# Attention scores issued before the PV that frees their slots, a PV that stops early, and a convolution that keeps instruction words in reserve

## The chip, the cores and the metric

One core of one Trainium2 chip runs the whole kernel. The metric is the device time of one execution in microseconds (us). The core has a tensor engine (PE; its weight loads are shown as PEld), a vector engine (DVE), a scalar engine (ACT), a general engine (POOL) and a queue engine (SP). The engines run their own instruction streams and wait for each other by semaphores.

## The reference

Two independent blocks share one launch, and their results stand side by side in the output. Block A is attention with 32 heads of 16 dimensions over 2048 rows; block B is a gated long convolution (written with FFTs in the reference, computed as a causal convolution here).

```python
# A: x (1, 2048, 512), wqkv (512, 1536), wo (512, 512), bfloat16
q, k, v = split_heads(x @ wqkv)                 # 32 heads, Dh = 16
scores = einsum("bhqd,bhkd->bhqk", q, k) * Dh ** -0.5
o = einsum("bhqk,bhkd->bhqd", softmax(scores), v)
a = merge_heads(o) @ wo
# B: q, k, v (1, 2048, 512), shift_k (512, 4), ssm_k (512, 2048), ssm_D (512)
kv = causal_conv4(k, shift_k) * v
y = causal_conv2048(kv, ssm_k) + kv * ssm_D
b = q * y
return concatenate([a, b], axis=-1)
```

The softmax needs 32 x 2048 x 2048 exponentials. They are the bulk of the work that is not matrix multiplication.

## The kernel before

**Tiles.** Attention is cut into 32 groups (8 groups of 4 heads by 4 blocks of 512 queries), each group into 16 key tiles of 128 and 4 heads: 2048 blocks of 128 keys by 512 queries. For one block PE computes the scores into one PSUM bank (`qk_mm`, L829), the exponential is taken, and PE multiplies the result with V (`emit_pv`, L966, called PV) and adds it into bank `PVB`. Four blocks whose heads lie in four different row strips make one set of four matmuls that run side by side.

**Two engines take exponentials.** ACT takes most blocks, two or three at a time (one instruction of 1024 or 1536 columns, L856, output in the ring `PT` of 19 slots). DVE takes the others by integer tricks: one pass out of PSUM (L892, output in the ring `PTD`), then three passes over two blocks together (L918, L923, L927).

**Steps.** The main loop counts steps `T`. A step issues the scores of its two or three ACT blocks and often of one DVE block (`emit_qk`), the ACT instruction that reads them, PV of blocks of two and more steps ago (`pv_step`), and then background work (`emit_bg`): the projections of Q, K, V and of the output, and the convolution (`conv_lags`, L1236), which is 8192 small matmuls in "lags" of four. Filler matmuls (`warm_up`, L1487) are put where PE would be idle for long, and `keep_busy` (L1493) once the convolution is done. The score banks are used in turns: the scores of step `T` wait until the ACT instruction of step `T-2` has read the same banks.

**The order is fixed when the program is built.** A planner in Python keeps a model of each engine's time and decides, step by step, what each engine's stream holds; nothing is decided on the chip. So a change of a rule moves instructions all through the program. Three rules matter here.

- `pv_make_room(T)` (L999): if one of the three `PT` slots that come next is still held by a block without its PV, PV is forced (`pv_step(T, True)`). The main loop calls it ahead of `emit_qk(T)`, so the forced PV stands before the scores of step `T` in PE's stream. Forced PV goes on through all blocks that are ready.
- `pv_step` without force issues every set of ready blocks that is full enough; nothing compares it with the time at which the next scores are due.
- PE's instructions arrive in blocks of 256 words (a matmul with its weight load is 2 words). The planner's model of PE (`Tensor`) notes when the next block is expected to land. `spare()` gives how many words of the present block may be used: what is left of it less `NEED` (12) words for each us until the landing. The convolution takes at most `spare() / 8` lags in a step, and the fillers ask it too.

Of the kernel before, what the change touches and what calls it, by code (L numbers as in the profile page):

```python
# [26 lines left out]
C = 512  # L27
# [11 lines left out]
PVB = 6  # L39
BGB = 7  # L40
# [3 lines left out]
LAGS = 14  # L44
# [17 lines left out]
N_TAIL = 10  # L62
# [3 lines left out]
R_PTD = 10  # L66
# [30 lines left out]
MARGIN = 0.2  # L97
QN_T = 4
PV_WAIT = 0.1
PV_AGAIN = 1  # L100
SPARE = 0
DMA_KB = 394
# [14 lines left out]
WAIT = 1  # L117
LATE = 0.2
V512 = (0.60, 0.726)
V4 = (0.20, 0.326), (0.334, 0.46)  # L120
V2 = (0.334, 0.46), (0.60, 0.726)
SAME = 0.012
SWITCH = 0.105
LANDS = 0.115
MM = 0.216
LAG = 0.0555
# [4 lines left out]
LOADED = 1.3  # L131
WR_KB = 310
NEED = 12.0
FILL = 0.054


# [73 lines left out]
class Tensor(Eng):  # L210
# [45 lines left out]
        end = max([b for a, b in self.loads[-12:] if a <= cross + ISSUED], default=0.0)  # L256
        return max(cross + FETCH, end + LOADED)

    def spare(self):
        need = max(self.lands - self.t, 0.0) * NEED  # L260
        return BLOCK - self.at_word % BLOCK - need if need else 10 ** 6


# [11 lines left out]
def bass_concat_heads__mha_block__ssm_conv_h3__prompt_kernel(  # L275
# [76 lines left out]
    pe = Tensor(sem("s_pe"), done)  # L352
# [3 lines left out]
    def at(*deps):  # L356
        return pe.at(deps)
# [127 lines left out]
    bank_free = {b: None for b in range(8)}  # L485
# [226 lines left out]
    NL = NQB * NG - 1  # L712
# [31 lines left out]
    late = {"bank": None}  # L744

    end = [10 ** 6]
# [27 lines left out]
    h_exp = {}  # L774
# [14 lines left out]
    def emit_qk(T):  # L789
        banks = take_banks(T)  # L790
        bl, extra = next_blocks(T, len(banks)) if len(queue) > LAST_BLKS else (queue[:2], None)
        d_bank = [hold(T, banks)] if extra is not None else []
        banks_of[T] = banks = banks[:len(bl)]
        chunks[T] = bl + [extra] * len(d_bank)
        for b in chunks[T]:
            queue.remove(b)
            chunk_of[b] = T
        on = list(zip(chunks[T], banks + d_bank))
        more = []
        if late["bank"] in banks and len(on) > 2:  # L800
            more = [on.pop(banks.index(late["bank"]))]
        h = qk_mm(on)
        if extra is not None:
            on_dve[extra] = len(on_dve)
            exp_on_dve(extra, d_bank[0], h)
        if more:
            if at(bank_free[more[0][1]]) + 0.13 > pe.t + 0.1:
                advance(pe.t)
                pv_take(T)
                pv_step(T)  # L810
            h = qk_mm(more)
        h_exp[T] = emit_exp(bl, banks, h)

    def qk_mm(on):
# [48 lines left out]
    pt_used, pt_of, pt_free = {}, {}, {}  # L863

    def pt_next():
        p = pt_at[0]
        return set(range(p, min(p + MOST, R_PT))) | (set(range(MOST)) if p + MOST > R_PT else set())
# [21 lines left out]
    def exp_on_dve(b, bank, h):  # L889
        i = on_dve[b]  # L890
        fix_u = PTD[:, i % R_PTD, 0, :].bitcast(U16)
        h_f = urgent(lambda e: e.tensor_scalar(fix_u, PS[:, bank, :], FIX_ADD, FIX_HI, ALU.add, ALU.min),  # L892
                     [h, h_ptd.get(i - R_PTD)], slack=S_FX)
        bank_free[bank] = h_f
        if waits and i % R_PTD:
            passes(waits.pop() + [b], i - 1, h_f)
        else:
            settle()
            waits.append([b])
            fixed[0] = h_f  # L900

    waits, fixed = [], [None]

    def settle():
        if waits:
            bl = waits.pop()
            passes(bl, on_dve[bl[0]], fixed[0])
# [29 lines left out]
    pv_n = {}  # L937
# [55 lines left out]
    def pv_make_room(T):  # L993
        pv_take(T)
        for i in range(2):
            p, need = pt_at[0], set()
            for n in (3,):
                p = 0 if p + n > R_PT else p
                need |= set(range(p, p + n))  # L999
                p += n  # L1000
            if not need & set(pt_used):
                return
            advance(pe.t)
            pv_step(T, True)

    acts, dves = [], []
    pv_seen = set()
# [12 lines left out]
            else:  # L1020
                acts.append((b, 0))

    def pv_step(T, force=False):
        pv_unit(T, force)
        if pv_part[0] is not None:
            return
        for n, j in sorted({sub(b) for b, part in acts + dves}):
            if n > 0 and pv_done.get(n - 1, T) >= T + force or j > 0 and not conv_done() or j > 1 and sub_done.get(j - 2, T) >= T:
                break
            a = [x for x in acts if sub(x[0]) == (n, j) and all((OF[n], kt // 4) in h_v for kt, q0, w in tiles(x[0]))]  # L1030
            d = [x for x in dves if sub(x[0]) == (n, j)]
            own = [i for i in range(4 * KT * n, 4 * KT * (n + 1)) if sub(i) == (n, j)]
            close = all(i in chunk_of for i in own) and T >= max(chunk_of[i] for i in own) + 2
            late = close and (T >= max(chunk_of[i] for i in own) + (NL_PV if n == NL and j < 3 else 2 if n == NL else LAST_PV) or force)
            if late:
                for b, part in d:
                    if b not in h_blk and waits and b in waits[0]:
                        settle()
                    while b not in h_blk:
                        k = dve.n  # L1040
                        advance(pick()[0] + 0.01)
                        assert dve.n > k
            d = [x for x in d if x[0] in h_blk and (late or at(h_blk[x[0]]) <= pe.t - (0.0 if close else LATE))]
            bl = a + d
            if bl and PV_WAIT and not force and n > 0 and T < end[0] - N_TAIL and not any(pv_n.get((n, i)) for i in range(4)) and at(bank_free[PVB]) + 0.13 > pe.t + pe.turn("C") + PV_WAIT:
                break
            while bl:
                run = []
                for x in bl:
                    if blk(x[0])[2] not in [blk(y[0])[2] for y in run]:  # L1050
                        run.append(x)
                old = [x for x in run if x[0] not in on_dve and pt_of[x[0]] in pt_next()]
                if len(run) < 4 and not close and not old and len([x for x in bl if x[0] in on_dve]) < DV_MIN and T < end[0]:
                    break
                for x in run:
                    bl.remove(x)
                    (dves if x[0] in on_dve else acts).remove(x)
                emit_pv(run, T)

    def finish_group(n, h, T):  # L1060
        dt = DT[:, :]
# [63 lines left out]
    h_wop = [None]  # L1125
# [168 lines left out]
    def room(T):  # L1294
        lim = at(h_exp[min(T, end[0] - 1)]) - 0.47 - MARGIN
        return lim - max(pe.t, at(bank_free[BGB]))
# [110 lines left out]
    def emit_bg(T):  # L1407
        st = state
        now[0] = T
        unit_step(T)  # L1410
        if T == N_OPEN:
            assert not early
            st["started"], st["t"] = True, pe.t
        if T >= end[0] - N_TAIL:
            tail_step(T)
            return
        if conv_done():
            if h_wop[0] is not None and not any(pv_n.get((NL, i, 128)) for i in range(4)):
                bank_free[BGB] = pe.op(keep_busy, [bank_free[BGB], h_wop[0]], run=MM, kind="F")
            return  # L1420
        if not st["started"] or alone[0] or at_rest() and (part[0] or st["turn"] or next_unit(T) is not None):
            return
        left_us = max(STEP_US * (PLAN - END - T) - JOB_US * len(jobs), 1.0)
        st["lags"] = min(st["lags"] + min(PACE * st["left"] / left_us, RATE) * (pe.t - st["t"]), CAP)
        st["t"] = pe.t
        left = min(LAGS, int(st["lags"]), int((room(T) - pe.turn("C") - SWITCH) / LAG), int(pe.spare() / 8))
        while left > 0 and st["qd"] < wr_next[0] and h_kvc[st["qd"] // 16] is not None and at(h_kvc[st["qd"] // 16]) + WAIT <= pe.t and at(h_wr[st["qd"]]) + WAIT <= pe.t:
            n0 = st["lag"]
            if n0 == 0 and st["qd"] % 4 == st["from"] and at(bank_free[BGB]) > pe.t - 0.2:
                break  # L1430
            n1 = min(n0 + left, NLAG)
            left -= n1 - n0
            st["lags"] -= n1 - n0
            st["left"] -= n1 - n0
            conv_lags(st["qd"], n0, n1)
            st["lag"] = n1 % NLAG
            if n1 == NLAG:
                st["qd"] += 1
                if st["qd"] % 4 == 0:
                    st["turn"] = True  # L1440
                if st["qd"] % 4 == st["from"]:
                    break
# [93 lines left out]
    T = 0  # L1536
    while T < end[0] + 3:
        if T < end[0]:
            pv_make_room(T)
            emit_qk(T)  # L1540
        advance(pe.t)
        alone[0] = full_step(T)
        pv_take(T)
        if not alone[0]:
            pv_step(T)
        advance(pe.t)
        emit_bg(T)
        warm_up(T)
        advance(pe.t)
        T += 1  # L1550
# [75 lines left out]
```

## Time and profile before

| | us |
|---|---|
| three timed executions | 749.92, 746.77, 749.25; median 749.25 |
| the profiled execution | 750.88 |
| its span, from the first to the last instruction | 749.1 |
| ACT busy in the span | 724.8 |
| PE busy, DVE busy | 703.4, 702.0 |

The mean granted TensorE clock is 0.991 of full speed. The profiled execution took 1.6 us more than the median. An engine's busy time is the union of its instructions; successive ACT instructions overlap in the records, so a sum of their durations is more than the busy time. A name such as "PT<-PS" says which tile is written and which is read.

### The profile page before, as it was taken

How to read it: one execution, taken by the hardware profiler on the slowest of the kernel's cores; microseconds unless marked ns; L12 is line 12 of the kernel's file. 1: busy time of each engine (PE TensorE's matmuls, PEld its weight loads, DVE VectorE, ACT ScalarE, POOL GpSimd, SP SyncE). 2: the span in 40 equal slices, each digit the busy share in tenths (PEclk: the TensorE clock that was granted, in tenths of full speed). 3: DMA queues.
4: the chain of work that ended last, by engine and by line, in shares of the span. 5: the costliest groups of instructions: out<-in, count | busy, mean ns of one | idle time of the engine just before them, and what ended most of it. 6: DMA issues, size and time to landing. Idle time of an engine off the chain costs nothing.

```text
span 749.1 us, 32530 instructions
## 1 busy us (share of the span) xinstructions
PE 703.4 (94%) x14696; PEld 315.4 (42%) x14696; DVE 702.0 (94%) x1437; ACT 724.8 (97%) x690; POOL 98.7 (13%) x172
## 2 busy tenths in 40 slices
PE   7999899999989999999999999999999999899997
PEld 3334344445443444444434344443443443344344
DVE  3999999999989999999899998999999997899995
ACT  6999999999989999999999999999999999899997
POOL 7202102020202002020021301120011201210000
PEclk9999999999999999999999999999999999999999
DMA  9797767677775787775576577575898566666210
GB/s 201 201 260 262 226 199 232 242 248 233 252 232 178 229 282 259 255 234 200 160 266 202 184 253 236 200 255 189 297 287 249 185 208 207 231 200 230 90 39 30
DMA packets 73720, 161.48 MB, mean 216 GB/s; under 512 B 34064, under 2 KB 37776, under 8 KB 73200
## 3 DMA queue, kind: packets, MB, share of 16 engines
q1 hardware_dynamic: 66400, 150.43, 62.0%
q0 software_dynamic: 5984, 8.66, 3.8%
q8 instruction: 116, 1.90, 1.0%
q10 hardware_dynamic: 1200, 0.33, 0.2%
q14 instruction: 20, 0.16, 0.1%
HBM read 142.61 MB, written 6.42 MB: 199 GB/s over the span
## 4 chain that ended last, share of the span: by engine, by line
ACT 60%; DVE 27%; PE 11%; issue 1%; DMA 1%; POOL 0%
ACT PT L856 60%; DVE PTD L892 11%; DVE PTD L923 5%; PE PS L829 4%; PE PS L966 4%; DVE PTD L918 3%; DVE PTD L927 3%; PE PS L1236 2%; DVE DT L1064 1%; DMA xT<-in_A_x_dram 1%; PE PS L516 1%; DVE KV L604 1%; PE PS L1493 1%; DVE OUTA L1149 1%; DVE QN L1271 0%
## 5 line engine op out<-in xcount | busy, mean ns | idle before, releaser
L856 ACT ACTIVATE PT<-PS 128x1024 bf16<-128x1024 f32 (+2 forms) x686 | 722.6, 1290 | 13.4 <-PE PS L829 13.0
L892 DVE TENSOR_SCALAR PTD<-PS 128x512 uint16<-128x512 f32 x464 | 309.8, 680 | 19.7 <-PE PS L829 18.6
L829 PE MATMUL PS<-QT,KTo 32*128 32x512 bf16 (+2 forms) x2248 | 271.6, 367 | 26.1 <-ACT PT L856 15.4
L966 PE MATMUL PS<-PT,VA 128*32 128x512 bf16 (+2 forms) x1748 | 181.2, 369 | 4.5 <-DVE PTD L923 1.4
L1236 PE MATMUL PS<-WR,KV 128*24 128x128 bf16 (+8 forms) x8192 | 182.6, 221 | 1.9 <-issue 1.9
L1236 PEld LDWEIGHTS PS<-WR,KV 128*32 128x32 bf16 (+7 forms) x8192 | 136.0, 95 | 58.7 <-issue 36.0
L923 DVE TENSOR_TENSOR PTD<-PTD 128x1024 f16<-128x1024 f16 x232 | 154.9, 678 | 0.3
L829 PEld LDWEIGHTS PS<-QT,KTo 32*128 32x128 bf16 x2248 | 71.2, 91 | 195.8 <-ACT PT L856 138.3
L966 PE MATMUL PS<-PTD,VA 128*32 128x512 f16 (+1 forms) x1000 | 152.9, 370 | 0.5 <-DVE PTD L927 0.4
L369 POOL DMA_DIRECT2D QT<-QS x120 | 61.2, 517 | 398.0 <-DVE QS L582 374.2
L927 DVE TENSOR_SCALAR PTD<-PTD 128x1024 uint16<-128x1024 uint16 x232 | 94.8, 414 | 0.3
L918 DVE TENSOR_SCALAR PTD<-PTD 128x1024 uint16<-128x1024 uint16 x232 | 92.2, 415 | 0.3
L966 PEld LDWEIGHTS PS<-PT,VA 128*32 128x32 bf16 x1748 | 45.6, 94 | 89.9 <-issue 71.0
L966 PEld LDWEIGHTS PS<-PTD,VA 128*32 128x32 bf16 x1000 | 38.6, 95 | 12.5 <-issue 1.6
L1487 PE MATMUL PS<-IDN,ZW 128*32 128x512 bf16 (+3 forms) x178 | 42.6, 307 | 0.3 <-DVE DT L1064 0.2
L369 POOL DMA_DIRECT2D out_dram<-OUTA x15 | 8.8, 586 | 109.3 <-DVE OUTA L1149 109.3
L1064 DVE STREAM_TRANSPOSE DT<-PS 128x512 f32<-128x512 f32 x31 | 21.9, 707 | 0.6 <-PE PS L966 0.5
L570 PE MATMUL PS<-WKV,xT 128*128 128x128 bf16 x256 | 19.3, 220 | 1.1 <-DVE KTo L591 0.5
L516 PE MATMUL PS<-xT,WQ 128*32 128x512 bf16 x240 | 18.3, 384 | 1.2 <-DVE DT L1064 0.7
L516 PE MATMUL PS<-xT,WKV 128*32 128x512 bf16 (+1 forms) x256 | 18.2, 376 | 0.8 <-DVE QN L1271 0.5
L1487 PEld LDWEIGHTS PS<-IDN,ZW 128*32 128x32 bf16 x178 | 13.2, 95 | 12.7 <-issue 8.1
L570 PEld LDWEIGHTS PS<-WKV,xT 128*128 128x128 bf16 x256 | 14.4, 98 | 8.8 <-issue 3.6
(72 smaller groups left out, 246.7 us busy)
## 6 DMA issues: line engine op xcount, KB each, us to landing
WR<-kz_scratch SPq DMA_DIRECT2D x256, 512.0 KB, 5.3
KV<-KV SPq DMA_DIRECT2D x16, 256.0 KB, 5.2
kz_scratch<-WR SPq DMA_DIRECT2D x1, 2176.0 KB, 8.3
QN<-in_B_q_dram POOLq DMA_DIRECT2D x8, 256.0 KB, 5.3
out_dram<-QN POOLq DMA_DIRECT2D x8, 256.0 KB, 2.9
QT<-QS POOLq DMA_DIRECT2D x120, 16.0 KB, 4.4
out_dram<-OUTA POOLq DMA_DIRECT2D x15, 128.0 KB, 2.7
QN<-in_B_ssm_k_dram SPq DMA_DIRECT2D x1, 1024.0 KB, 8.0
```

The costliest lines, as they stand in the source:

```text
L369: f(outp, inp).then_inc(dsem.sem, 16)
L516: ins = e.matmul(dst[g:g + 32], lhsT=w[:, g:g + 32], rhs=rhs, tile_position=(0, g), **kw)
L570: ins = e.matmul(PS[:, bank, 128 * j:128 * j + 128], lhsT=xT[:, dc, (4 * sc + j) * 128:(4 * sc + j + 1) * 128], rhs=WV[:, dc, o * 128:(o + ...
L829: ins = e.matmul(PS[:, bank, i * w:i * w + w], lhsT=KTo[32 * s:32 * s + 32, OF[n_] % 2, kt * 128:(kt + 1) * 128], rhs=QT[32 * s:32 * s + 3 ...
L856: h = act.op(lambda e: e.activation(PT[:, p0:p0 + n, :], src, ACT.Exp, scale=EXP_SCALE, bias=EXP_BIAS), [h, free], us=(0.065 + 0.4257 * n, ...
L892: h_f = urgent(lambda e: e.tensor_scalar(fix_u, PS[:, bank, :], FIX_ADD, FIX_HI, ALU.add, ALU.min), [h, h_ptd.get(i - R_PTD)], slack=S_FX)
L918: st["h"] = dve.op(lambda e: e.tensor_scalar(mant_u, fix_u, MANT, HALF_BITS, ALU.bitwise_and, ALU.bitwise_or), [st["h"]], us=us)
L923: st["h"] = dve.op(lambda e: e.tensor_tensor(mant, fix, mant, ALU.mult), [st["h"]], us=us)
L927: h = dve.op(lambda e: e.tensor_scalar(fix_u, fix_u, OCTAVE, ONE_MORE, ALU.bitwise_and, ALU.bitwise_or), [st["h"]], us=us)
L966: ins = e.matmul(dst, lhsT=w, rhs=rhs, start=first, stop=last, tile_position=(0, 32 * s))
L1236: ins = e.matmul(PS[32 * g:32 * g + 2 * ((30 - d) // 2 + 1), BGB, 128 * kk:128 * kk + w], lhsT=kv, rhs=WR[:, r + g, S - 64 * d - 128:S - 6 ...
L1487: pe.op(lambda e, s=s, k=k, rhs=rhs, bank=bank, rows=rows, c0=c0, first=first: e.matmul(PS[32 * s:32 * s + rows, bank, c0:c0 + 128 * k], l ...
```

## The change

- `pv_make_room(T)` moves out of the main loop into `emit_qk`: now behind the scores of step `T` and ahead of the ACT instruction that writes into the freed slots. Forced PV stops as soon as the slots are free (`enough`).
- `pv_step` without force returns when the next set of PV would put PE's time more than `PV_OVER` (0.2 us) past the time at which the scores that follow are due by the model.
- The convolution's reserve is `NEED_C` = 17 words for each us to the landing instead of 12. The fillers keep 12.
- `keep_busy` is put in only if its bank is free already.
- The passes of DVE blocks are written for a general number of blocks together, `WIDE`. It is 2, as before, and the first two entries of the planner's tables `V4` and `V2` are the old ones to a thousandth.

```diff
+PV_OVER = 0.2
+WIDE = 2
+NEED_C = 17.0
@@ Tensor
-    def spare(self):
-        need = max(self.lands - self.t, 0.0) * NEED
+    def spare(self, rate=NEED):
+        need = max(self.lands - self.t, 0.0) * rate
@@ emit_qk
             h = qk_mm(more)
+        pv_make_room(T)
         h_exp[T] = emit_exp(bl, banks, h)
@@ exp_on_dve
-        if waits and i % R_PTD:
-            passes(waits.pop() + [b], i - 1, h_f)
-        else:
+        if waits and i % R_PTD == 0:
             settle()
-            waits.append([b])
-            fixed[0] = h_f
+        if not waits:
+            waits.append([])
+        waits[0].append(b)
+        fixed[0] = h_f
+        if len(waits[0]) == WIDE:
+            settle()
@@ pv_make_room
-            pv_step(T, True)
+            pv_step(T, True, lambda: not need & set(pt_used))
@@ pv_step
-    def pv_step(T, force=False):
+    def pv_step(T, force=False, enough=lambda: False):
...
+                if not force and not late and T < end[0] - N_TAIL and max(pe.t, at(bank_free[PVB]) if not any(pv_n.get((n, i)) for i in range(4)) else 0.0) + pe.turn("C") + MM > at(h_exp[T]) - 0.47 + PV_OVER:
+                    return
...
                 emit_pv(run, T)
+                if enough():
+                    return
@@ emit_bg
-            if h_wop[0] is not None and not any(pv_n.get((NL, i, 128)) for i in range(4)):
+            if h_wop[0] is not None and not any(pv_n.get((NL, i, 128)) for i in range(4)) and at(bank_free[BGB]) <= pe.t:
...
-        left = min(LAGS, int(st["lags"]), int((room(T) - pe.turn("C") - SWITCH) / LAG), int(pe.spare() / 8))
+        left = min(LAGS, int(st["lags"]), int((room(T) - pe.turn("C") - SWITCH) / LAG), int(pe.spare(NEED_C) / 8))
@@ main loop
-            pv_make_room(T)
             emit_qk(T)
```

What this does to the streams can be read from the built programs. L829 and L966 of before are L833 and L972 in the changed kernel, L1236 is L1246, and L1487 is L1497.

The first place is PE's stream where PV is forced, some 543 us into the span of the kernel before. QT,KTo names scores, WR,KV the convolution, PT,VA and PTD,VA are PV of ACT's and of DVE's blocks.

```order
L829 MATMUL PS<-QT,KTo 128x512 x3
L1236 MATMUL PS<-WR,KV 16x128 x4
L1236 MATMUL PS<-WR,KV 14x128 x8
L1236 MATMUL PS<-WR,KV 12x128 x8
L1236 MATMUL PS<-WR,KV 10x128 x8
L1236 MATMUL PS<-WR,KV 8x128 x4
L966 MATMUL PS<-PT,VA 32x512 x15
L966 MATMUL PS<-PTD,VA 32x512 x5
L829 MATMUL PS<-QT,KTo 128x512 x3
L1236 MATMUL PS<-WR,KV 8x128 x4
```

One of the forced PVs in PE's stream of the changed kernel:

```order
L833 MATMUL PS<-QT,KTo 128x512 x3
L1246 MATMUL PS<-WR,KV 22x128 x4
L1246 MATMUL PS<-WR,KV 20x128 x8
L1246 MATMUL PS<-WR,KV 18x128 x8
L1246 MATMUL PS<-WR,KV 16x128 x8
L1246 MATMUL PS<-WR,KV 14x128 x8
L833 MATMUL PS<-QT,KTo 128x512 x3
L972 MATMUL PS<-PT,VA 32x512 x12
L1246 MATMUL PS<-WR,KV 12x128 x8
```

Before, 32 matmuls of the convolution and 20 of PV stand between two sets of scores. Now only the convolution does, and PV follows the scores. The ACT instruction of that step waits for the first four PV matmuls behind its scores, which free its slots. Eight ACT instructions of the changed kernel wait in this way; in the kernel before none waits for a PV.

The second place lies two steps behind the first difference of the two programs (there the convolution's 12x128 x8 was taken out): PE's stream where the kernel before is some 87 to 92 us into its span. IDN,ZW names fillers. Before:

```order
L829 MATMUL PS<-QT,KTo 128x512 x3
L966 MATMUL PS<-PT,VA 32x512 x2
L966 MATMUL PS<-PTD,VA 32x512 x2
L829 MATMUL PS<-QT,KTo 128x512 x6
L966 MATMUL PS<-PT,VA 32x512 x5
L966 MATMUL PS<-PTD,VA 32x512
L1236 MATMUL PS<-WR,KV 10x128 x4
L829 MATMUL PS<-QT,KTo 128x512 x6
L966 MATMUL PS<-PT,VA 32x512 x3
L966 MATMUL PS<-PTD,VA 32x512
L966 MATMUL PS<-PT,VA 32x512
L966 MATMUL PS<-PTD,VA 32x512 x3
```

The same place in the changed kernel:

```order
L833 MATMUL PS<-QT,KTo 128x512 x3
L972 MATMUL PS<-PT,VA 32x512 x2
L972 MATMUL PS<-PTD,VA 32x512 x2
L833 MATMUL PS<-QT,KTo 128x512 x6
L972 MATMUL PS<-PT,VA 32x512 x5
L972 MATMUL PS<-PTD,VA 32x512
L1246 MATMUL PS<-WR,KV 12x128 x4
L833 MATMUL PS<-QT,KTo 128x512 x3
L1497 MATMUL PS<-IDN,ZW 32x512
L1497 MATMUL PS<-IDN,ZW 32x256
L833 MATMUL PS<-QT,KTo 128x512 x3
L972 MATMUL PS<-PT,VA 32x512 x3
```

The convolution is two lags (8 matmuls, 12x128) later here, and two fillers stand between two sets of scores that followed each other directly.

Over the whole program these counts differ: ACT instructions of 1024 columns 477 before and 473 after, of 1536 columns 206 and 210; DVE blocks 464 and 460; PV matmuls of 512 columns 2428 and 2424; fillers 178 and 226; `keep_busy` matmuls 20 and 6. Scores, projections, convolution and DMAs are the same in number.

More of the change, by code (lines that the diff above doesn't have):

```diff
@@ L119 @@
 V512 = (0.60, 0.726)
-V4 = (0.20, 0.326), (0.334, 0.46)
-V2 = (0.334, 0.46), (0.60, 0.726)
+WIDE = 2
+V4 = [(0.067 + 0.1333 * n, 0.193 + 0.1333 * n) for n in (1, 2, 3, 4)]
+V2 = [(0.067 + 0.2667 * n, 0.193 + 0.2667 * n) for n in (1, 2, 3, 4)]
 SAME = 0.012
```

## The prediction

> **What bounds the kernel now.** I read the page's first part, the chain that ended last, the groups of instructions with their shapes kept apart, and then ACT's instructions in order of time, which show every place where ACT stood idle.
>
> ```profile
> span 749.1 us, 32530 instructions
> PE 703.4 (94%) x14696; PEld 315.4 (42%) x14696; DVE 702.0 (94%) x1437; ACT 724.8 (97%) x690; POOL 98.7 (13%) x172
> ACT 60%; DVE 27%; PE 11%; issue 1%; DMA 1%; POOL 0%
> L856 ACT ACTIVATE PT<-PS 128x1024 bf16<-128x1024 f32 (+2 forms) x686 | 722.6, 1290 | 13.4 <-PE PS L829 13.0
> ...
> L856 ACT ACTIVATE PT<-PS 128x1024 bf16<-128x1024 f32 x477 | 467.4, 1159 | 12.5 <-PE PS L829 12.3
> L892 DVE TENSOR_SCALAR PTD<-PS 128x512 uint16<-128x512 f32 x464 | 309.8, 680 | 19.7 <-PE PS L829 18.6
> L856 ACT ACTIVATE PT<-PS 128x1536 bf16<-128x1536 f32 x206 | 303.3, 1586 | 0.3 <-PE PS L829 0.2
> ```
>
> ACT is busy 97% of the span and carries most of the chain. Its exponentials are nearly fixed work, so what can be won is the time in which ACT waits for scores: 13.0 us are visible, all released by PE's scores (L829). DVE and PE at 94% have little more room, so a gain for ACT comes only from a better order, not from work that moves to them.
>
> The visible gaps are not all. 686 instructions of 1290 ns are 884.9 us, yet they cover 722.6; so two that follow each other without a gap overlap by about 162/662 = 0.24 us. A late set of scores first eats this overlap, so I charge each gap 0.24 us more than its row shows.
>
> The rows of ACT in order of time: start, length of a piece without a gap, and in brackets the idle time ahead of it.
>
> ```profile
> 94.45 117.71 ACT L856 ACTIVATE PT<-PS 128x1024 bf16<-128x1024 f32 x112 [0.29 <-PE PS L829]
> 214.17 1.02 ACT L856 ACTIVATE PT<-PS 128x1024 bf16<-128x1024 f32 x1 [2.01 <-PE PS L829]
> 215.78 1.02 ACT L856 ACTIVATE PT<-PS 128x1024 bf16<-128x1024 f32 x1 [0.59 <-PE PS L829]
> 217.12 8.29 ACT L856 ACTIVATE PT<-PS 128x1024 bf16<-128x1024 f32 x8 [0.31 <-PE PS L829]
> 225.66 51.42 ACT L856 ACTIVATE PT<-PS 128x1536 bf16<-128x1536 f32 x49 [0.25 <-PE PS L829]
> 277.31 36.70 ACT L856 ACTIVATE PT<-PS 128x1024 bf16<-128x1024 f32 x35 [0.23 <-PE PS L829]
> 314.33 23.33 ACT L856 ACTIVATE PT<-PS 128x1024 bf16<-128x1024 f32 x22 [0.31 <-PE PS L829]
> 338.56 10.12 ACT L856 ACTIVATE PT<-PS 128x1024 bf16<-128x1024 f32 x10 [0.91 <-PE PS L829]
> 349.01 39.99 ACT L856 ACTIVATE PT<-PS 128x1024 bf16<-128x1024 f32 x37 [0.33 <-PE PS L829]
> 389.55 38.72 ACT L856 ACTIVATE PT<-PS 128x1024 bf16<-128x1024 f32 x37 [0.54 <-PE PS L829]
> 429.11 67.80 ACT L856 ACTIVATE PT<-PS 128x1024 bf16<-128x1024 f32 x65 [0.85 <-PE PS L829]
> 497.61 44.36 ACT L856 ACTIVATE PT<-PS 128x1024 bf16<-128x1024 f32 x43 [0.70 <-PE PS L829]
> 543.30 40.06 ACT L856 ACTIVATE PT<-PS 128x1024 bf16<-128x1024 f32 x38 [1.33 <-PE PS L829]
> 583.70 1.02 ACT L856 ACTIVATE PT<-PS 128x1024 bf16<-128x1024 f32 x1 [0.34 <-PE PS L829]
> 585.21 4.32 ACT L856 ACTIVATE PT<-PS 128x1024 bf16<-128x1024 f32 x4 [0.48 <-PE PS L829]
> 590.13 39.08 ACT L856 ACTIVATE PT<-PS 128x1024 bf16<-128x1024 f32 x36 [0.60 <-PE PS L829]
> 651.26 1.02 ACT L856 ACTIVATE PT<-PS 128x1024 bf16<-128x1024 f32 x1 [1.31 <-PE PS L829]
> 652.45 1.02 ACT L856 ACTIVATE PT<-PS 128x1024 bf16<-128x1024 f32 x1 [0.17 <-PE PS L829]
> 653.91 60.15 ACT L856 ACTIVATE PT<-PS 128x1024 bf16<-128x1024 f32 x57 [0.44 <-PE PS L829]
> ```
>
> I looked at PE ahead of each and found two kinds. **Held by PV** are the seven gaps at 225.66, 314.33, 338.56, 429.11, 497.61, 543.30 and 590.13: 12 to 20 matmuls of PV stand between two sets of scores, at six of them behind convolution as well. They sum to 4.95 us, with 7 x 0.24 to 6.6 us. **Held by fetch or clock** are the other twelve: 2.91 (214 to 217), 0.23, 0.33, 0.54, 0.82 (583 to 585), 1.92 (651 to 654) and 0.29 (94.45), together 7.0 us, with 12 x 0.24 to 9.9 us. PE at the largest gap of the first kind:
>
> ```profile
> 540.51 0.63 PE L1236 MATMUL PS<-WR,KV 128*16 128x128 bf16 x32
> 541.67 1.04 PE L966 MATMUL PS<-PT,VA 128*32 128x512 bf16 x15 [0.53 <-DVE QS L582]
> 542.34 0.59 PE L966 MATMUL PS<-PTD,VA 128*32 128x512 f16 x5
> 542.86 0.39 PE L829 MATMUL PS<-QT,KTo 32*128 32x512 bf16 x3
> ```
>
> Convolution ends at 541.14, PV waits 0.53 us for DVE, then runs, and only at 542.86 the scores follow that ACT has needed since 541.97 (543.30 less 1.33). PE and the clock at gaps of the second kind:
>
> ```profile
> q8 instruction: 116, 1.90, 1.0%
> PEld PS L1236 <- issue: 36.0, 147, 2.1
> 213.13 0.45 PE L1236 MATMUL PS<-WR,KV 128*16 128x128 bf16 x15 [1.92 <-issue]
> 90.61 0.61 PE L829 MATMUL PS<-QT,KTo 32*128 32x512 bf16 x3 [0.53 <-DVE PTD L918]
> 213.00:217.00 4.00, 3.87 (x66) 1.52 (x66) 2.24 (x4) 2.05 (x2) 0.00 (x0) 0.57 0.42 103
> 90.00:92.00 2.00, 1.48 (x14) 0.24 (x11) 2.00 (x5) 2.00 (x3) 0.00 (x0) 0.62 0.11 37
> 582.00:586.00 4.00, 4.00 (x73) 1.80 (x66) 3.30 (x7) 3.18 (x4) 0.00 (x0) 0.57 0.00 0
> ```
>
> At 213.13 PE stood 1.92 us in the middle of a run of convolution with no semaphore to wait for. The instruction queue moved 1.90 MB in 116 packets for PE's 29,392 instructions: 65 bytes each, some 253 in a packet. A late packet fits that stop. The stops ahead of 277.31, 349.01, 389.55 and 651.26 look alike. And a stop is paid twice: in the four us from 213 the granted clock is 0.57, a set of scores takes 0.61 instead of 0.39 us, and ACT's next gaps (0.59, 0.31) are the price. At 90.6 and 582 the clock falls without a packet being late, behind shorter idle times of PE.
>
> **The change part by part, against the profiled execution's 750.9 us.**
>
> ACT's work: four blocks move from DVE to ACT (206 to 210 wide instructions, 477 to 473 narrow ones). Each costs 1586 - 1159 = 427 ns: **+1.7 us**, on the path. DVE is spared four passes of 680 ns and more behind them; off the path, nothing.
>
> Forced PV behind the scores, and PV that stops: the new order has no place where 12 or more PV matmuls stand between convolution and the next scores, so I let all seven holds go: **-6.6 us**. What is late next is the PV itself: eight ACT instructions wait for four PV matmuls that stand behind their scores. Queued behind these on PE is the rest of PV or convolution, and the next scores, which have a whole ACT instruction (0.9 us and more) to come. At 541 the first PV could start at 541.67 because of DVE; four matmuls later, by the starts at 541.67 and 542.34 for 15 of them about 0.2 us, ACT would be released near 542.1 to 542.2, against 541.97: a gap of 0.2 instead of 1.33. Bounds for the eight: nothing, where PV is free to run, and 0.71 us each, the 0.53 of this row and the 0.2 of PV fully exposed: 5.7 us. I take 0.2 each, the row I have: **+1.5 us**.
>
> The larger reserve: with 3 us to the landing, 15 words more stay for others, which is a set of scores and a PV set (7 matmuls, 14 words), one step of about 0.9 us. That shortens the stops at 214 and 651 by 0.9 us each: -1.8. At 94.45 (0.29 and 0.24) two fillers now stand where PE idled 0.53 us ahead of 90.61; if the clock holds there, -0.5. Together **-2.3 us**. Bounds: all twelve gone, -9.9; or one more stop of the largest kind, since every packet now ends at another instruction, +3.6 (2.91 and 3 x 0.24). I stay near the small end because the other rows show no convolution ahead of the stop.
>
> The Trainium skill (Runtime: NRT & Kernel Launch, Instruction fetch mechanics) says that the next 16 KiB block is fetched while the present one is executed, and that fetching is hidden because instructions are dispatched more slowly than the block fills. This trace agrees on the size (1.90 MB in 116 packets) and not on the hiding, if the 1.92 us are such a stop. By that rule the reserve is worth nothing, and the sum is the second rival's.
>
> At nothing: the passes in `WIDE` (464 and 460 blocks, in twos as before), the new gate on `keep_busy` (20 to 6 matmuls, so the convolution ends some 14 steps later, under cover of the steps that are still left before the tail), and the WR and QT loads, whose number is unchanged; they are issued at other times because the convolution moves, which is part of the fetch term's bounds.
>
> Sum: 750.9 + 1.7 - 6.6 + 1.5 - 2.3 = 745.2. The profiled execution is 1.6 us above the median of 749.25, and the three timed ones spread over 3.2 us, about one large stop. I take half of the 1.6 off: **744.3 us**.
>
> **Rivals.**
>
> 1. The reserve changes nothing, since stops come from elsewhere or only move. For it: no convolution ahead of some stops. 744.3 + 2.3 = 746.6.
> 2. The hold is only renamed: ACT waits for PV as long as it waited for scores. For it: PV's own wait for DVE (0.53) stays. Against it: only four of up to 20 matmuls stand in the way. All eight at 0.71: 744.3 + 4.2 = 748.5. That the change doesn't do what it says ends here too.
> 3. Slower: scores go out earlier, PV and convolution hold back, and PE idles more in a step, so that the clock falls at more places than the four of before. Each costs 0.34 + 0.48 + 2 x 0.24 = 1.3 us, as at 583. Four more eat the gain; from eight on (+10.4) it is 754.7, slower by more than 0.5%. For it: at 90.6 idle times of about half a us were enough. Against it: 178 fillers become 226.
> 4. Nearly all stops vanish: 744.3 - 7.6 = 736.7.
>
> The Trainium skill (TensorE: Matmul & The Clock Gate, Part 1) lets the clock fall to half only after an idle window of about 3.4 us. Here 0.57 follows 1.92 us of idling, and 0.62 a mere 0.53, so the measurement speaks against it. By that rule the third rival would have no price and its chance would go to the forecast.
>
> **How the numbers follow.** Forecast 0.58, by itself 741 to 747.5; of it I put 0.46 under 745.5 and 0.12 above. First rival 0.16, second 0.10, third 0.06, fourth 0.10 (737 to 741). 0.5% of 749.25 is 3.75 us, about what a measurement of this kernel can tell from no change. Faster 0.46 + 0.10 = 0.56, same 0.12 + 0.16 + 0.10 = 0.38, slower 0.06. The range from 738.5 to 749.5 takes in the second rival and most of the fourth and leaves out the third.
>
> **What would show it.** Right: ACT's idle time before its exponentials falls from 13.0 to 6 us or so; none of its gaps has 12 PV matmuls ahead of the scores; some small gaps are released by PV (L972) instead of scores; 210 wide instructions. The reserve: the longest stop without a releaser stays under 2.1 us, and fewer windows show a clock near 0.57. Wrong: gaps near 0.7 us released by PV; or more windows of low clock with PE idle ahead of them; or a total of ACT's gaps that stays at 13 us with stops at new places.

## The result and the profile after

| | before | after |
|---|---|---|
| median, us (6 runs each) | 749.59 (746.73 to 750.15) | 741.65 (739.65 to 744.61) |
| profiled execution, us | 750.88 | 741.82 |
| its span | 749.1 | 739.5 |
| mean granted clock | 0.991 | 1.000 |

The ratio is 0.9909 with a 95% interval of 0.9881 to 0.9937: faster by 0.6 to 1.2%.

The page of the changed kernel, first part, chain and the group of the exponentials:

```profile
PE 699.4 (95%) x14719; PEld 316.5 (43%) x14726; DVE 697.2 (94%) x1426; ACT 724.9 (98%) x690; POOL 97.6 (13%) x172
ACT 84%; PE 10%; DVE 5%; DMA 1%; issue 1%; POOL 0%
L860 ACT ACTIVATE PT<-PS 128x1024 bf16<-128x1024 f32 (+2 forms) x686 | 722.7, 1314 | 3.2 <-PE PS L833 2.9
```

ACT's busy time is what it was (722.7 against 722.6), though it does four blocks more: they are paid by more overlap, since fewer gaps cut the stream. The idle time that scores end fell from 13.0 to 2.9 us, and the chain runs through ACT for 84% instead of 60%. ACT in order of time, after; the bracket is the idle time ahead of the piece:

```profile
9.09 236.74 ACT L860 ACTIVATE PT<-PS 128x2048 bf16<-128x2048 f32 x223 [1.03 <-PE PS L833]
246.49 42.41 ACT L860 ACTIVATE PT<-PS 128x1024 bf16<-128x1024 f32 x40 [0.66 <-PE PS L833]
289.08 30.16 ACT L860 ACTIVATE PT<-PS 128x1024 bf16<-128x1024 f32 x29 [0.17 <-PE PS L833]
319.68 62.94 ACT L860 ACTIVATE PT<-PS 128x1024 bf16<-128x1024 f32 x59 [0.44 <-PE PS L833]
383.24 350.72 ACT L860 ACTIVATE PT<-PS 128x1536 bf16<-128x1536 f32 x335 [0.62 <-PE PS L833]
```

Of 23 gaps five are left, one of them at the start. The last piece runs 350 us and 335 instructions without a gap. Three of the five (246.49, 319.68, 383.24) follow a stop of PE that no semaphore ended; the largest of these on PE, and the waits of PE's weight loads that nothing released:

```profile
245.29 0.40 PE L972 MATMUL PS<-PT,VA 128*32 128x512 bf16 x4 [0.75 <-issue]
```

```profile
PEld PS L972 <- issue: 75.8, 322, 1.2
PEld PS L1246 <- issue: 29.0, 128, 0.2
```

The columns of the second are sum, times and longest, in us. In the convolution the longest such wait was 2.1 us before and is 0.2 now. The clock in the four us where it had been low before (213) and in another such stretch (582):

```profile
213.00:217.00 4.00, 3.87 (x54) 1.52 (x54) 4.00 (x9) 4.00 (x5) 0.00 (x0) 1.00 0.86 331
582.00:586.00 4.00, 4.00 (x151) 2.38 (x140) 4.00 (x10) 4.00 (x4) 2.71 (x6) 1.00 0.98 308
```

The number ahead of the last two is the granted clock: full speed, and so it is throughout.

### The profile page after: what moved, and what is told of

It is laid out like the page before. It is cut to its first block, busy times and chain, and to the rows that moved or that the text cites. A ratio compares the mean times of both kernels' runs of the same rounds, so it can differ in the third digit from the quotient of the medians.

```text
span 739.5 us, 32574 instructions
## 1 busy us (share of the span) xinstructions
PE 699.4 (95%) x14719; PEld 316.5 (43%) x14726; DVE 697.2 (94%) x1426; ACT 724.9 (98%) x690; POOL 97.6 (13%) x172
## 4 chain that ended last, share of the span: by engine, by line
ACT 84%; PE 10%; DVE 5%; DMA 1%; issue 1%; POOL 0%
ACT PT L860 84%; PE PS L833 3%; PE PS L972 3%; PE PS L1246 2%; DVE PTD L896 2%; PE PS L519 1%; DVE PTD L929 1%; DMA xT<-in_A_x_dram 1%; DVE PTD L924 0%; PE PS L573 0%; PE PS L695 0%; DVE PTD L933 0%; DVE KTo L594 0%; DVE QN L1281 0%; DVE VA L624 0%
## 5 line engine op out<-in xcount | busy, mean ns | idle before, releaser
L860 ACT ACTIVATE PT<-PS 128x1024 bf16<-128x1024 f32 (+2 forms) x686 | 722.7, 1314 | 3.2 <-PE PS L833 2.9
L833 PE MATMUL PS<-QT,KTo 32*128 32x512 bf16 (+2 forms) x2248 | 269.3, 365 | 21.6 <-ACT PT L860 11.8
L972 PE MATMUL PS<-PT,VA 128*32 128x512 bf16 (+2 forms) x1752 | 183.7, 367 | 3.3 <-DVE VA L624 1.8
L1246 PE MATMUL PS<-WR,KV 128*28 128x128 bf16 (+8 forms) x8192 | 183.2, 219 | 0.2
L1246 PEld LDWEIGHTS PS<-WR,KV 128*24 128x24 bf16 (+7 forms) x8192 | 136.3, 95 | 55.4 <-issue 29.0
L972 PE MATMUL PS<-PTD,VA 128*32 128x512 f16 (+1 forms) x992 | 153.2, 367 | 1.2 <-issue 0.8
L833 PEld LDWEIGHTS PS<-QT,KTo 32*128 32x128 bf16 x2248 | 70.7, 91 | 185.8 <-ACT PT L860 137.0
L933 DVE TENSOR_SCALAR PTD<-PTD 128x1024 uint16<-128x1024 uint16 x230 | 93.6, 413 | 0.2
L924 DVE TENSOR_SCALAR PTD<-PTD 128x1024 uint16<-128x1024 uint16 x230 | 91.4, 416 | 0.3
L972 PEld LDWEIGHTS PS<-PT,VA 128*32 128x32 bf16 x1752 | 45.5, 94 | 90.2 <-issue 71.7
L1497 PE MATMUL PS<-IDN,ZW 128*32 128x128 bf16 (+3 forms) x226 | 50.7, 302 | 0.1
L972 PEld LDWEIGHTS PS<-PTD,VA 128*32 128x32 bf16 x992 | 39.6, 95 | 13.7 <-issue 4.1
L1497 PEld LDWEIGHTS PS<-IDN,ZW 128*32 128x32 bf16 x226 | 16.5, 95 | 15.9 <-issue 9.5
L372 POOL DMA_DIRECT2D out_dram<-QN x8 | 6.1, 763 | 103.5 <-PE PS L972 50.7
```

Source lines behind the costliest of these rows:

```text
L372: f(outp, inp).then_inc(dsem.sem, 16)
L833: ins = e.matmul(PS[:, bank, i * w:i * w + w], lhsT=KTo[32 * s:32 * s + 32, OF[n_] % 2, kt * 128:(kt + 1) * 128], rhs=QT[32 * s:32 * s + 3 ...
L860: h = act.op(lambda e: e.activation(PT[:, p0:p0 + n, :], src, ACT.Exp, scale=EXP_SCALE, bias=EXP_BIAS), [h, free], us=(0.065 + 0.4257 * n, ...
L924: st["h"] = dve.op(lambda e: e.tensor_scalar(mant_u, fix_u, MANT, HALF_BITS, ALU.bitwise_and, ALU.bitwise_or), [st["h"]], us=us)
L933: h = dve.op(lambda e: e.tensor_scalar(fix_u, fix_u, OCTAVE, ONE_MORE, ALU.bitwise_and, ALU.bitwise_or), [st["h"]], us=us)
L972: ins = e.matmul(dst, lhsT=w, rhs=rhs, start=first, stop=last, tile_position=(0, 32 * s))
```

## The experiments

Each line of results is the median of a kernel's runs and its ratio to the kernel before on the same chip, with the 95% interval.

**The parts one by one.** Three kernels make one part of the change each in the kernel before; a fourth takes the reserve out of the changed kernel.

The order alone, without `enough` (the run also lets `pv_make_room` force PV up to eight times instead of two; the built program is the same with two):

```diff
+        pv_make_room(T)
         h_exp[T] = emit_exp(bl, banks, h)
...
-            pv_make_room(T)
             emit_qk(T)
```

> The kernel before with forced PV moved behind the scores alone; forced PV goes on through all that is ready, the reserve stays 12. Theory A: the seven holds go and some small waits for PV come (at most 1.5 us in all), the stops and the low clock stay; 744 to 747 us. Rival (the hold is only renamed): gaps released by PV of 0.7 us each, 748 to 750 us.

Measured: 748.17 us, 0.9997 (0.9975 to 1.0020). ACT's waits in its profiled run, which was the fastest of its ten (745.58):

```profile
ACT PT L857 <- PE PS L830: 4.8, 11, 1.2
ACT PT L857 <- PE PS L967: 1.4, 3, 0.6
```

That is above the 744 to 747 us of Theory A. The mechanism is as expected: no PV of 12 or more matmuls stands between convolution and scores any longer (7 places before), three gaps are released by PV (L967) with 0.6 us at most, and the sum fell from 13.0 to 6.2 us. But the median gained nothing. PE's stops remain (1.19 us at 212, 0.98 us at 479 in this run), and the times spread from 745.58 to 750.97. That stops, which vary from run to run, take back what the holds gave is argued, since only the fastest run has a profile.

The stop of unforced PV alone, with forced PV still ahead of the scores:

```diff
+                if not force and not late and T < end[0] - N_TAIL and max(pe.t, at(bank_free[PVB]) if not any(pv_n.get((n, i)) for i in range(4)) else 0.0) + pe.turn("C") + MM > at(h_exp[T]) - 0.47 + PV_OVER:
+                    return
```

> The kernel before with the stop of unforced PV alone (0.2 us past the due time); forced PV still ahead of the scores. Theory A: PV that is held back comes back as forced PV ahead of scores, so the holds stay at 5 us or grow; 748 to 752 us. Rival (the stop is what removed the holds): holds gone, 744 to 746 us.

Measured: 747.49 us, 0.9980 (0.9949 to 1.0011), just under the range of Theory A. The order has 8 places of the old kind, one more than before (near 702.8 us, where ACT stood idle for 0.48 us), and ACT waited 11.8 us for scores. The stop does not remove the holds.

The reserve alone:

```diff
-        left = min(LAGS, int(st["lags"]), int((room(T) - pe.turn("C") - SWITCH) / LAG), int(pe.spare() / 8))
+        left = min(LAGS, int(st["lags"]), int((room(T) - pe.turn("C") - SWITCH) / LAG), int(pe.spare(NEED_C) / 8))
```

> The kernel before with the convolution's reserve of 17 words alone. Theory A (the reserve keeps PE from running dry at the end of a block of instruction words): the gaps that PV holds stay (about 5 us visible), the stops of PE without a releaser and the windows of low clock get fewer; 743 to 746 us. Theory B (the stops vanished in the changed kernel only because all instructions moved): as many stops as before at other places, within 2 us of the kernel before. A and B are told apart by the stops in the trace more than by the time.

Measured: 751.70 us, 1.0038 (1.0014 to 1.0062), slower, so both theories missed. ACT's waits, its two largest gaps, and PE ahead of the second of them:

```profile
ACT PT L857 <- PE PS L830: 14.3, 18, 2.0
```

```profile
133.09 13.30 ACT L857 ACTIVATE PT<-PS 128x1024 bf16<-128x1024 f32 x13 [1.74 <-PE PS L830]
...
249.26 12.39 ACT L857 ACTIVATE PT<-PS 128x1024 bf16<-128x1024 f32 x12 [2.02 <-PE PS L830]
```

```profile
248.05 0.83 PE L967 MATMUL PS<-PT,VA 128*32 128x512 bf16 x12 [1.13 <-DVE DT L1065]
248.82 0.39 PE L830 MATMUL PS<-QT,KTo 32*128 32x512 bf16 x3
```

PV ahead of the scores waited 1.13 us for DVE, and the scores behind it were late by two us. Low clock is gone (mean 0.999), but six stops of 0.4 to 1.4 us are left, five of them ahead of a PV matmul. They were to tell the theories apart: six stops of 5.9 us in all, against four of 3.5 us before, are nearer to Theory B. So with the reserve by itself low clock went and the stops did not, and the holds got longer (six gaps of 6.0 us in all, against seven of 5.0).

The changed kernel with the old reserve:

```diff
-NEED_C = 17.0
+NEED_C = 12.0
```

> The changed kernel with the reserve back at 12 words. Theory A: holds stay away, stops and low clock come back: 744 to 748 us, three or more stops over 0.5 us or windows of low clock. Theory B (the reserve does nothing): 740 to 743 us, as the changed kernel.

Measured: 750.21 us, 1.0033 (0.9999 to 1.0066): somewhat later than expected, and Theory B falls. Its ACT and PE:

```profile
582.98 1.02 ACT L860 ACTIVATE PT<-PS 128x1024 bf16<-128x1024 f32 x1 [2.14 <-PE PS L833]
...
710.85 1.94 ACT L860 ACTIVATE PT<-PS 128x1024 bf16<-128x1024 f32 x2 [3.39 <-PE PS L833]
```

```profile
PEld PS L972 <- issue: 81.5, 324, 3.8
```

Seven stops of 0.3 us or more, 9.3 us together, the longest 3.3 us; and the clock is 0.993 on average again. The holds stay away, but all that they gave is lost to stops.

**Blocks of instruction words.** Is a stop really the end of a block whose successor has not landed? The changed kernel again, and two with the whole stream of PE moved by 128 words. In the first the planner does not count the shift, so the order is that of the changed kernel to the last instruction and only the block boundaries lie elsewhere in it; in the second it does, and lays a new order.

```diff
-        for _ in range(8):
-            ins = e.matmul(PS[:, 0, :], lhsT=PT[:, 0, 0:128], rhs=PT[:, 0, 0:512], start=True, stop=True)
+        for _ in range(72):
+            ins = e.matmul(PS[:, 0, 0:64], lhsT=PT[:, 0, 0:128], rhs=PT[:, 0, 0:64], start=True, stop=True)
...
     pe.op(warm, [h_w0], run=2.6, kind="F")
+    pe.at_word -= 128
```

The last line is in the first of the two alone.

> The changed kernel once more, so that the next three stand beside it on one chip. Every theory: about 0.99 of the kernel before.

> The changed kernel, every engine in the same order, but the 8 warm-up matmuls of 512 columns at the start are 72 of 64 columns, so all later instructions of PE lie 128 words further, half a block, and the planner is not told of it. Theory A (PE stops when a block of 256 words is used up before the next has landed, and the order is laid around the boundaries): the reserve now stands at the wrong places; more and longer stops, 5 to 10 us more than the changed kernel, 746 to 752 us. Theory B (blocks don't matter, the changed kernel gains by its order of scores and PV alone): as the changed kernel within 2 us.

> The same 72 short warm-up matmuls, but the planner counts them, so it lays a new order around the true boundaries. Theory A: as the changed kernel, 739 to 744 us, with few stops; a new order alone costs nothing. Rival (any new order loses what this one gained by luck): 745 us or more.

Measured: 740.75 us, 0.9889 (0.9845 to 0.9932); 787.69 us, 1.0511 (1.0445 to 1.0577); 743.81 us, 0.9925 (0.9898 to 0.9952). The untold shift, in a profile of the slowest of its four runs: its chain, ACT's waits, PE's waits in the convolution and one stop:

```profile
ACT 44%; PE 35%; DVE 14%; issue 5%; DMA 2%; SPq 1%; POOL 0%
```

```profile
ACT PT L861 <- PE PS L834: 43.7, 50, 2.6
PEld PS L1247 <- issue: 60.6, 154, 2.6
```

```profile
113.60 0.38 PE L1247 MATMUL PS<-WR,KV 128*2 128x128 bf16 x8 [2.31 <-issue]
113.92 0.61 PE L834 MATMUL PS<-QT,KTo 32*128 32x512 bf16 x3
```

The same instructions in the same order cost 47 us more when their boundaries move by half a block, where Theory A had expected 5 to 10; 28 stops of 0.3 us or more sum to 32.4 us, and the clock falls to 0.972 on average in this run. Once the planner counts the shift it costs little (0.9925 beside 0.9889). So the stops are block ends, the order is laid around them, and a second order laid in this way gains too.

The instruction queue's packets (q8) say the same. In the traces of all fourteen runs, each of the 77 stops of 0.3 us or more (idle times of PE that no semaphore ended, without the last 9 us) ends 1.2 to 1.6 us behind the landing of such a packet, though the packets are some 6 us apart. Whether a block has landed in time is not fixed by the order: the changed kernel's two profiled runs have three stops each (1.9 and 1.8 us in all), and only the first stands at the same instruction.

**How wide a reserve.** The changed kernel with 15 and 20 words, and the told shift with 12:

```diff
-NEED_C = 17.0
+NEED_C = 15.0
```

(20.0 and 12.0 in the other two.)

> The changed kernel with a reserve of 15 words, between 12 (750.2) and 17 (740.8). Theory A: between them, 742 to 747 us. Rival (luck of the order): anything from 740 to 752 us, not in step with the reserve.

> The changed kernel with a reserve of 20 words. Theory A: a wider reserve keeps the stops away as well, 739 to 744 us. Rival (17 is a lucky order): 745 us or more, with stops over 0.5 us.

> The order with 72 short warm-up matmuls that the planner counts, with the reserve at 12 words: the second pair of orders that differ in the reserve alone. Theory A (the reserve itself is worth several us): 2 to 8 us slower than with 17 words (743.8), with more stops of PE. Rival (each new order has its own luck, the reserve is worth little on average): 741 to 746 us.

| reserve, words per us | 12 | 15 | 17 | 20 |
|---|---|---|---|---|
| order of the change, us | 750.21 | 747.49 | 740.75, 741.65 | 745.09 |
| ratio to before | 1.0033 | 0.9986 | 0.9889, 0.9909 | 0.9954 |
| told shift, us (ratio) | 749.64 (1.0011) | | 743.81 (0.9925) | |
| fillers in the order | 172; 177 shifted | 176 | 226; 226 shifted | 228 |

In both orders 12 words lose some 6 to 9 us against 17, and 15 lies between, half a us above what was expected. 20 came out slower than expected, as the rival (17 is a lucky order) had it: its profiled run has a stop of 2.27 us at 517 and a low clock behind it. Each number of the table is one order or two, so steps of three or four us may be the luck of an order. That 12 is worse than 17 was seen twice, and the opposite once: in the kernel before, the reserve alone cost 3.1 us (751.70 against 748.61).

**The stop of PV and the fillers, taken out of the changed kernel.**

```diff
-PV_OVER = 0.2
+PV_OVER = 99.0
```

> The changed kernel without the stop of unforced PV (the limit is 99 us). Theory A: forced PV stays behind the scores, but unforced PV of 12 to 16 matmuls delays scores a little in many steps: 1 to 4 us more than the changed kernel, 742 to 745 us. Rival (the stop does nothing): as the changed kernel within 1 us.

Measured: 744.96 us, 0.9962 (0.9929 to 0.9995), some 3 to 4 us more than the changed kernel, at the upper end of the expectation. Alone the stop was worth nothing that could be told from none; with the others it may pay, but a step of this size may also be the luck of an order.

```diff
-            if k < 1 or lately > BUSY * WINDOW or pe.spare() < 2:
+            if k < 1 or lately > BUSY * WINDOW or pe.spare() < 2 or N_OPEN < T < end[0] - N_TAIL:
```

> The changed kernel without fillers between the opening and the last ten steps. If idle PE lowers the clock (windows near 0.57 behind idle times of half a us): several such windows, 1.3 us each, 743 to 752 us. If only stops lower it: as the changed kernel within 2 us, no such window.

This leaves out the fillers between the opening and the last steps; 33 of 226 remain.

Measured: 749.37 us, 1.0016 (0.9979 to 1.0053), mean clock 0.988. PE at the second place that the section on the change shows, in the changed kernel and then without fillers:

```profile
90.68 0.39 PE L833 MATMUL PS<-QT,KTo 32*128 32x512 bf16 x3
91.00 0.50 PE L1497 MATMUL PS<-IDN,ZW 128*32 128x512 bf16 x2
91.60 0.39 PE L833 MATMUL PS<-QT,KTo 32*128 32x512 bf16 x3
```

```profile
90.66 0.39 PE L833 MATMUL PS<-QT,KTo 32*128 32x512 bf16 x3
91.58 0.59 PE L833 MATMUL PS<-QT,KTo 32*128 32x512 bf16 x3 [0.52 <-DVE PTD L924]
```

```profile
91.00:95.00 4.00, 3.48 (x32) 0.71 (x33) 3.69 (x9) 4.00 (x5) 0.00 (x0) 0.58 0.03 9
214.00:218.00 4.00, 4.00 (x94) 2.16 (x87) 3.43 (x7) 3.34 (x4) 0.00 (x0) 0.57 1.03 402
```

The scores lie at the same times to 0.02 us. With two fillers (of 512 and 256 columns) between them the second set takes 0.39 us; without them it takes 0.59 us and the next 3.4 us run at half clock, as they did in the kernel before at 90.6.

## Why the prediction was right, step by step

The forecast of 744.3 us, faster, held: 741.65, inside its range. Its steps did not all have the right size, and there is luck in the sum: the term that most of it rests on (-6.6 for the holds) gained no time by itself, and the one kept small (-2.3 for the reserve) came out larger.

- **The bound** was read rightly. ACT's work stayed, and nearly all that was gained is ACT's waiting: 10.1 us of visible gaps, and 18 gaps fewer at 0.24 us of eaten overlap are 4.3 more. Against these 14.4 us stand 1.7 for the four blocks and 0.5 for a later start (the first exponential at 9.09 instead of 8.10, half of it counted as a gap already); the span fell by 9.6. The other 2.6 us sit in delays shorter than the overlap, which show as no gap: by the distances between ACT's starts (0.904 us behind an instruction of 1024 columns and 1.331 behind one of 1536 where nothing delays the next), steps without a gap lost 7.3 us before and 9.8 after.
- **The holds by PV** (-6.6) went as forecast: of seven gaps none is left with 12 PV matmuls behind convolution; 0.17 at 289.08 is the one gap that PV and a projection still make. The order alone removes the same holds without the other parts, but its median of 748.17 us does not show the 6.6 us.
- **The new waits for PV** (+1.5) show in no row of ACT in the changed kernel: the eight waits take up to 0.35 us each from the overlap, 1.4 us in all by the distances between ACT's starts, which is the size forecast (eight at 0.2 us are 1.6, not the 1.5 of the sum). With the order alone, which has no `enough`, three became gaps of up to 0.6 us. The second rival, that the hold is only renamed, is refuted.
- **The larger reserve** is the term that was mis-sized: -2.3 stood in the sum, and of 9.9 us in twelve gaps three gaps are left, 1.72 us and 3 x 0.24, so about -7.5. I had let two stops shrink by 0.9 us each, at 214 and 651; the profile puts the second, 1.41 us on PE, down to DVE. In fact all four windows of low clock went, and four stops became three shorter ones (3.5 us to 1.9). What I had missed is that the reserve works through the fillers too: words that the convolution leaves let them in (172 and 177 in the two orders with 12 words, 226 in both with 17), and fillers keep the clock. I had counted that at one place only, 94.45, where it went as forecast. That all of the -7.5 is the reserve's is not shown: the fastest run of the order alone, with 12 words, has no low clock either, and 17 words without fillers took 749.37 us, much as 12 words with theirs (750.21).
- **The first rival**, that the reserve changes nothing, falls with 12 words in the changed kernel (+8.6 us against 741.65) and in the told shift (+5.8), though in the kernel before the reserve's sign was the other. The Trainium skill (Runtime: NRT & Kernel Launch, Instruction fetch mechanics), from which it came, has fetching hidden by slow dispatch; the untold shift, with 28 stops at block ends, disagrees by 47 us. (Without the reserve's term the sum is this rival's, 746.6, not the second's, as the prediction has it.)
- **The third rival**, a falling clock, is real as a mechanism and was kept away by fillers: without them the kernel is as slow as the one before. The Trainium skill (TensorE: Matmul & The Clock Gate, Part 1) asks for an idle window of about 3.4 us; here idle times of 0.95 and 0.52 us within two us, with little work around them, were enough, though the low stretch itself lasts 3.4 us (91.6 to 95.0), which fits its window. These idle times alone do not decide, however: the order alone has the same two, ahead of 88.87 and 90.71, and its clock stayed full. In each trace the low stretches begin whole multiples of 3.41 us apart, as if PE's busy time were summed in windows of that length. In the kernel before they begin at 90.47, 213.35, 581.99 and 650.26, behind windows in which PE was busy 61, 44, 63 and 47% of the time. The window ahead of the fall without fillers, and the two windows of the order alone, between which the same idle times are shared out:

```profile
88.23:91.64 3.41, 1.90 (x26) 0.57 (x22) 3.41 (x9) 3.41 (x5) 0.00 (x0) 1.00 0.60 219
```

```profile
85.49:88.91 3.42, 2.47 (x40) 0.80 (x32) 3.42 (x8) 3.42 (x5) 1.16 (x2) 1.00 1.00 370
88.91:92.32 3.41, 2.48 (x30) 0.67 (x30) 3.41 (x8) 3.41 (x4) 0.00 (x0) 1.00 0.09 28
```

PE (the second number) was busy 56% of the first window and 72 to 73% of the others; with the two fillers of the changed kernel it is 71%. In the fourteen traces 28 low stretches begin, 27 of them behind a window with PE busy at most 65%; of some 2900 windows behind which none begins, 17 are as low.

- **That terms add** was assumed and is wrong. Alone, the three parts gave ratios of 0.9997, 0.9980 and 1.0038; together 0.9909, and without the reserve 1.0033. Why the reserve alone is slower was not tried further. Five of its six stops stand ahead of PV, so a burst of forced PV (12 to 20 matmuls, 24 to 40 words) may use up what the convolution left; that is argued, not shown.

## What to carry to other kernels

Where instructions are fetched in blocks and one engine runs thousands of short ones, look for idle times without a releaser, count the instructions between them, and keep long runs of cheap instructions from using a block up before the next lands; a planner that knows the boundaries is worth checking by moving the boundaries and not the work. Put what the bound engine needs ahead of what merely frees room for it, and stop the latter when there is room. Parts of such a change have to be tried together as well as alone, since one may spend what another has saved, and one new order is one draw.

## What the runs showed of the hardware

- Half a block of instruction words (128 of 256) of displacement, with the same order behind the warm-up, cost 6% (787.69 against 740.75 us).
- PE's clock fell to half for 3.4 us, or a multiple of it, at the end of windows of 3.41 us in which PE had been busy 32 to 70% of the time. No long idle time was needed, and the same idle times of 0.95 and 0.52 us did or did not lower the clock. Two filler matmuls in a gap of half a us raised the share from 56 to 71%, and the clock stayed full.
- Each of 77 stops of PE without a semaphore ended 1.2 to 1.6 us behind the landing of a packet of instructions.
- A stop of 1.9 us cost ACT 2.9 us of visible gaps (214 to 217 before): 2.01 at the stop, and 0.59 and 0.31 while the clock was at half behind it (213.35 to 216.76) or just after.
